# A Fourier mixing and maxout kernel on one core: one more split unit a batch, fewer and larger x fetches, evenly spaced scattered stores, and a re-cut first stage

## The chip, the cores and the metric

One NeuronCore of a Trainium2 chip runs the whole kernel. The metric is the device time of one execution in microseconds (us); lower is better. Five engines matter: TensorE (PE, matmuls into PSUM), VectorE (DVE), ScalarE (ACT), GpSimd (POOL), and SyncE (SP), which only issues DMAs here. POOL issues the loads of x and of the weights, which cast fp32 to bf16 on the way, and the scattered stores.

## The reference

x is 8 batches of 3072 rows of 256 numbers. The real part of a two-dimensional Fourier transform (over the 3072 rows and the 256 columns) is taken of each batch, and every resulting row of 256 goes through a maxout network with three input matrices and one output matrix.

```python
def _attn_ref(x):                      # x: (8, 3072, 256)
    X = np.fft.fft(x, axis=1)
    X = np.fft.fft(X, axis=2)
    return X.real.astype(np.float32)

def _moe_ref(x, w1, w2, w3, w_out):    # x: (24576, 256), w1..w3: (256, 768), w_out: (768, 256)
    h = np.maximum(np.maximum(x @ w1, x @ w2), x @ w3)
    return (h @ w_out).astype(np.float32)
```

Inputs and output are fp32; the kernel computes in bf16 with fp32 sums.

## The kernel before

**Algebra.** The transform over rows is done in two steps. Step s (`Mix.s`, lines 392 to 412) multiplies slices of x with a small table `tab`. The result goes through DRAM and back (`y`, `z`), or, for batch 0, through one DVE transpose (`t`, line 429). Step k (`Mix.k`, lines 456 to 466) multiplies with the tables `te_tab` and `to_tab` and gives `tE` and `tO`, the even and odd halves of the transform. Rows n and 3072 - n of the output share them, as a sum and a difference, so one unit of work makes both. The transform over the 256 columns is folded into the weights: `g_all` holds, for each of six chunks of 128 hidden columns, w2 - w1 and w3 - w1 in that form, even and odd part each, and `gd_all` holds multiples of the odd parts by a factor per partition (`dif`). Adding `gd_all` x `tO` to a plus sum turns it into the minus sum. `gw` and `g1t` carry the linear part (w1), which goes straight to the output.

**Units.** Each batch has 1536 row pairs in three blocks of 512 and six hidden chunks, so 18 units, numbered u = 0 to 17 inside a batch and g over all 144. The main loop (lines 880 to 917) takes one unit a turn. `begin` computes the plus side into `hp`, `finish` the minus side into `hm`, one unit later. There are two ways to do it:

- An unsplit unit has six matmuls of 512 columns: two each for two banks in `begin` (lines 485 and 486), and two in `finish` (line 492). ACT takes relu of one bank (`stmp`, line 498) and DVE the maximum with the other (line 499), once for each side.
- A split unit has five. `third`, called two units ahead, computes the even and the odd part of the w3 side into banks of their own (e and d, lines 841 and 843). ACT copies the odd part (line 845), DVE adds the correction `vb` x `wcol` to the even part (line 846), and POOL forms `plus` and `minus` in SBUF (line 850). `begin` then has two matmuls (lines 860 and 861) and `finish` one, and DVE takes both maxima (lines 862 and 874).

From g = 7 on, odd units are split. Even units are split where `EXTRA` says so, from batch 1 on: u = 0, 4, 8, and in the last batch also 14. The correction column `wcol` is made once, in unit 5 of batch 0 (`column`, lines 345 to 355), by 24 matmuls of one column.

**Second layer.** When a block's six chunks are done, `l2_block` is queued, and each unit runs ten steps of it, so a block's output appears during the next six units. DVE adds (line 577) into one of three output buffers (`obuf` and two halves of `kq`). Rows that lie regularly go out by SP (line 507). The mirrored rows go out as indirect stores issued by POOL (`scatter`, line 653), five per batch, which the main loop takes from the list `waiting`: one each at u = 8, 10 and 12 and two at u = 14. The last block of the last batch (`l2_last`, lines 584 to 617) is computed in flipped order instead, so that it needs no scatter; POOL makes the flipped tables (line 893) at unit 12.

**Plan.** Everything else is hung on units by `at(b, unit, fn)`: the k, s, y and z steps of the next batch, the loads of x three batches ahead, and the mirror copies of x (line 128, on ACT from batch 2 on, eight chunks at u = 5 to 12), which need both halves of the load (32 partitions each). The order of each engine's instructions is the order of this program; every queue is in order.

**First stage.** x of batch 0 comes in four chunks. DVE mirrors each (line 128); column 0 of the mirror is a copy of its own (line 132), by ACT for the first three chunks and by DVE for the last. s5 and s6 follow, DVE casts (line 403), DVE transposes, and then `m.k(0, 0, dve)` and `m.k(1, 0)` give the first 512 columns of `tE` (cast by DVE) and `tO` (cast by ACT), each in one PSUM bank of the pool `ps_f`. The pool `ps_s` of five banks serves this stage alone; the banks of the pools `ps_l1`, `ps_w3` and `ps_o`, which the units use, take its place afterwards.

**PSUM.** `ps_f` has three banks that e, d, the s and k steps and the linear part share in turn; `ps_l1` and `ps_o` have two each, `ps_w3` one. An even unit uses the `ps_w3` bank: as its second bank when it is unsplit, as its only one when it is split.

Of the kernel before, what the change touches and what calls it, by code (L numbers as in the profile page):

```python
# [9 lines left out]
FP32 = mybir.dt.float32  # L10
BF16 = mybir.dt.bfloat16
INT32 = mybir.dt.int32
UINT32 = mybir.dt.uint32
AX = mybir.ActivationFunctionType
# [13 lines left out]


FIRST_OF = (4, 8, 1)  # L30
EXTRA, EXTRA_LAST = (0, 4, 8), (0, 4, 8, 14)


def _parts(g):

    done = [(12 + i - 1, slice(128 * i + 96, 128 * i + 128)) for i in range(4)]
    for i in range(4 if g < 2 else 3):
        done.append((FIRST_OF[g] + i - 1, slice(128 * i, 128 * i + 96)))
    if g == 2:
        done += [(16, slice(384, 480, 2)), (15, slice(385, 480, 2))]  # L40
    return done
# [3 lines left out]
def kernel(  # L45
# [9 lines left out]
    nc = tc.nc  # L55

    B, S, D = x.shape
    assert (S, D) == (3072, 256)
    DFF = moe_w1.shape[1]
# [4 lines left out]
    NS = 49  # L64
# [6 lines left out]
    consts = ctx.enter_context(tc.tile_pool(name="consts", bufs=1))  # L71
# [20 lines left out]
    te_tab = consts.tile([128, NHALF + 1], BF16, tag="te_tab")  # L92
    to_tab = consts.tile([128, NHALF + 1], BF16, tag="to_tab")
    md_all = consts.tile([128, 512], BF16, tag="md_all")
    nmd_all = consts.tile([128, 512], BF16, tag="nmd_all")
    md = [md_all[:, fc * 256:(fc + 1) * 256] for fc in range(2)]
    nmd = [nmd_all[:, fc * 256:(fc + 1) * 256] for fc in range(2)]
    w1_bf = consts.tile([128, 2 * DFF], BF16, tag="w1_bf")
    w2_bf = consts.tile([128, 2 * DFF], BF16, tag="w2_bf")
    w3_bf = consts.tile([128, 2 * DFF], BF16, tag="w3_bf")  # L100
    wout_bf = consts.tile([128, NJC * 256], BF16, tag="wout_bf")
    g1t = consts.tile([128, NJC * 256], BF16, tag="g1t")
    g_all = consts.tile([128, 4 * DFF], BF16, tag="g_all")
    g_all = g_all.rearrange("p (c k j) -> p c k j", k=4, j=128)
# [11 lines left out]
    def load_x(b, s0, s1, h):  # L116

        rows = x[b].rearrange("(a s) d -> a s d", s=96)
        lo, hi = (s0, s1) if h == 0 else (max(s0, 1), min(s1, 48))
        src = rows[:, lo:hi, :] if h == 0 else rows[:, 97 - hi:97 - lo, :][:, ::-1, :]  # L120
        return nc.gpsimd.dma_start(out=xt[b % 2][32 * h:32 * h + 32, lo:hi, :], in_=src)  # L121

    def mirror(b, s0, s1):

        t = xt[b % 2]
        fn = (nc.vector.tensor_copy, (nc.gpsimd.tensor_copy, nc.vector.tensor_copy)[s0 >= 25],
              nc.scalar.copy)[min(b, 2)]
        fn(out=t[64:128, s0:s1, 1:128], in_=t[0:64, s0:s1, 255:128:-1])  # L128
        if b < 2:
            if b == 0 and s0 < 40:  # L130
                fn = nc.scalar.copy
            fn(out=t[64:128, s0:s1, 0], in_=t[0:64, s0:s1, 128])

    def mirror_first(b):

        t = xt[b % 2]
        nc.scalar.copy(out=t[64:128, :, 0], in_=t[0:64, :, 128])
# [3 lines left out]
    ps_s = ps_s_cm.__enter__()  # L141
# [52 lines left out]
    zero = gen.tile([128, 512], BF16, tag="zero")  # L194
    nc.vector.memset(zero, 0.0)
    nc.vector.memset(x0u, 0.0)
    half_pi = gen.tile([128, 1], FP32, tag="half_pi")
    nc.vector.memset(half_pi, 0.5 * math.pi)
    nc.scalar.activation(out=half_pi, in_=half_pi, func=AX.Sin)
# [4 lines left out]
    turn = gen.tile([128, 2], FP32, tag="turn")  # L204
# [10 lines left out]
    def scal(out, in0, s1, op0, s2=None, op1=None, eng=None):  # L215
        kw = {} if op1 is None else {"op1": op1}
        return (eng or nc.vector).tensor_scalar(out=out, in0=in0, scalar1=s1, scalar2=s2,
                                                op0=op0, **kw)
# [37 lines left out]
    dve = nc.vector.tensor_copy  # L256
    vm = gen.tile([128, 512], INT32, tag="vm")
# [16 lines left out]
    def wrap(c0, c1):  # L274
# [8 lines left out]
                          in_=par.unsqueeze(1).to_broadcast([128, 2, 2]))  # L283
# [42 lines left out]
    def differ(i0, i1, j0, j1):  # L326

        cs = slice(j0 // 128, j1 // 128)
        nc.vector.tensor_scalar(out=gd_all[:, cs, i0:i1, :], in0=g_all[:, cs, 2 * i0 + 1:2 * i1:2, :],
                                scalar1=dif, scalar2=None, op0=ALU.mult)  # L330
# [14 lines left out]
    def column():  # L345

        psc = ps_f.tile([128, 512], FP32, name="psc", tag="ps")
        for jc in range(NJC):
            for k, (table, wt) in enumerate(((md, w3_bf), (nmd, w1_bf))):
                for fc in range(2):  # L350
                    nc.tensor.matmul(psc[:, jc:jc + 1],
                                     wt[:, fc * DFF + jc * 128: fc * DFF + jc * 128 + 128],
                                     table[fc][:, 128:129],
                                     start=(k == 0 and fc == 0), stop=(k == 1 and fc == 1))
        nc.scalar.copy(out=wcol, in_=psc[:, 0:NJC])

    def prep_second():
# [143 lines left out]
    def stored(st, mine, others):  # L501
        for group in others:
            tc.declare_no_dep(st.ins, group=group, reason="each store has rows of its own")
        tc.add_to_no_dep_group(mine, st.ins)
# [144 lines left out]
    def scatter(n):  # L649

        for _ in range(min(n, len(waiting))):
            row, col, p0, p1, src = waiting.pop(0)
            stored(nc.gpsimd.indirect_dma_start(  # L653
                fours, bass.IndirectOffsetOnAxis(ap=rows_m[p0:p1, col:col + 1], axis=0),
                src, None, element_offset=256 * row), "scattered", ("scattered", "direct"))
            nc.gpsimd.memset(mark, 0.0)
# [11 lines left out]
    def warm_up(n):  # L668
        for _ in range(n):
            nc.tensor.matmul(warm, zero[:, 0:128], zero, start=True, stop=True)  # L670

    m = Mix(0)
# [11 lines left out]
    mirror(0, *FIRST[3])  # L684
    m.s(4, pool=ps_s)
    warm_up(2)
    scal(sgn, pidx, 0.0, ALU.is_equal)
    scal(sgn, sgn, 2.0, ALU.mult, -1.0, ALU.add)
    scal(dif, sgn, 1.0, ALU.subtract)
    m.s(5, pool=ps_s, evict=dve)  # L690
    nc.scalar.activation(out=md_all, in_=vm, func=AX.Sin, scale=float(2.0 * math.pi / 256.0),
                         bias=turn[:, 0:1])
    m.s(6, pool=ps_s)
    m.t()
    warm_up(2)
    nc.scalar.activation(out=nmd_all, in_=vm, func=AX.Sin, scale=float(-2.0 * math.pi / 256.0),
                         bias=turn[:, 1:2])
# [4 lines left out]
    for (s0, s1) in HALVES:  # L702
        for h in range(2):
            load_x(1, s0, s1, h)
        if s0 == 0:
            nc.gpsimd.dma_start(out=wout_bf.rearrange("p (jc c) -> p jc c", jc=NJC),
                                in_=moe_w_out.rearrange("(jc p) c -> p jc c", jc=NJC))
# [8 lines left out]
    table(1, 512, 1024)  # L716
    m.c(1, 16)
    warm_up(1)
    m.k(0, 0, dve)
    m.k(1, 0)  # L720
    differ(0, 2, 0, 128)
    keep(psg2, 1, 2, 128, 384, dve)
    differ(0, 2, 128, 384)
# [32 lines left out]
    def at(b, unit, fn):  # L756
        plan.setdefault((b + unit // UNITS, unit % UNITS), []).append(fn)
# [23 lines left out]
    def fetch(b, k):  # L781
        half, h = divmod(k, 2)
        load_x(b, *HALVES[half], h)

    def turn(b, ch):
        mirror(b, *EIGHTHS[ch])
# [14 lines left out]
        at(0, (3, 3, 4, 4)[ch], lambda ch=ch: mirror(1, *CHUNKS[ch]))  # L801
        at(0, 4, lambda ch=ch: fetch(2, ch))
    for b in range(2, B):
        for ch in range(4):
            if b > 2:
                at(b - 3, (9 + (b == 3), 11, 18, 19)[ch], lambda b=b, ch=ch: fetch(b, ch))
        for ch in range(8):
            at(b - 2, 5 + ch + 3 * (b == 2), lambda b=b, ch=ch: turn(b, ch))
        at(b - 2, 13 + 3 * (b == 2), lambda b=b: mirror_first(b))
# [70 lines left out]
    for g in range(B * UNITS):  # L880
        b, u = divmod(g, UNITS)
        blk, jc = divmod(u, NJC)
        mm = mixes[b]
        last = b == B - 1 and blk == 2
        if jc == 0:
            hp = h_pool.tile([128, NJC, TOKB], BF16, name="hp", tag="hp")
            hm = h_pool.tile([128, NJC, TOKB], BF16, name="hm", tag="hm")
            if last:
                flipped = []
                for t, name in ((mm.tE, "tEr"), (mm.tO, "tOr")):  # L890
                    fl = h_pool.tile([128, TOKB], BF16, name=name, tag=name)
                    flipped.append(fl)
                    nc.gpsimd.tensor_copy(fl, t[:, 3 * TOKB - 1: 2 * TOKB - 1: -1])
        if prev is not None and is_split(prev[0]) and not is_split(g):
            finish(*prev)
            prev = None
        pses = begin(g, hp[:, jc, :])
        if prev is not None:
            finish(*prev)
        prev = (g, pses, hm[:, jc, ::-1] if last else hm[:, jc, :])  # L900
        for lead in (1, 2):
            if is_split(g + lead) and (lead == 1) == (g + lead == 7):
                third(g + lead)
        scatter({8: 1, 10: 1, 12: 1, 14: 2}.get(u, 0))
        l2_some(10)
        if b == B - 1 and u in (1, 3):
            if u == 1:
                middle = l2_mid()
            next(middle, None)
        for fn in plan.get((b, u), ()):  # L910
            fn()
        if jc == NJC - 1:
            l2_some(1000)
            if g == B * UNITS - 1:
                finish(*prev)
            l2_queue.append(l2_last(hp, hm, mm.tE, mm.tO, flipped) if last else
                            l2_block(b, blk, hp, hm, mm.tE, mm.tO))
# [32 lines left out]
```

## Time and profile before

| what | value |
|---|---|
| median of 3 runs | 392.28 us (392.26 to 392.38) |
| the profiled execution | 391.42 us, its span 389.3 us |
| mean granted TensorE clock | 0.998 |
| PE busy | 376.2 us (97% of the span) |
| DVE, POOL, ACT busy | 327.7, 314.3, 248.4 us |
| one batch in the middle | 44.28 us |
| POOL plus and minus, each | 1.27 us, 91 of each |
| scattered stores on POOL | 37, 1.0 us each |

The span runs from the first to the last instruction; the execution's time has 2.1 us around it. A matmul's row shows its whole passage through the array (380 ns for 512 columns), and consecutive ones overlap, so what a matmul costs is read from start to start. A row of the timeline gives start, duration, engine, line, operation, output and inputs; the bracket at its end is the idle time of that engine before it and what ended it.

### The profile page before, as it was taken

Reading aid. Unit: us, or ns where it says so; the run is one execution under the profiler, and the core shown is the slowest. Engines: PE = TensorE matmul, PEld = TensorE weight load, DVE = VectorE, ACT = ScalarE, POOL = GpSimd, SP = SyncE. Lnnn points to the kernel's source line nnn. Section 1 sums busy time; section 2 is a strip of 40 time slices with the busy share of each in tenths; the row PEclk is TensorE's granted clock in tenths of the full one; section 3 lists DMA queues with packets and bytes.
Section 4 is the critical chain, followed back from the end, with each engine's and each line's share of the span. In section 5 each row is a group of like instructions: output and inputs, shape, how many; then the busy total and the mean of one; then the engine's idle time right before and its main releaser. Section 6 shows DMA issues by size and latency. Waiting matters only on the chain.

```text
span 389.3 us, 8092 instructions
## 1 busy us (share of the span) xinstructions
PE 376.2 (97%) x2817; PEld 236.2 (61%) x2817; DVE 327.7 (84%) x552; ACT 248.4 (64%) x453; POOL 314.3 (81%) x363
## 2 busy tenths in 40 slices
PE   6699999999999999999999999999999999999985
PEld 2355566566665666566665666656665666666654
DVE  7788797799797988899797988989887997999972
ACT  6877789567856696567856687567866346434420
POOL 9983576879898898879898898879787887769881
PEclk9999999999999999999999999999999999999999
DMA  7999764585747666475938657575423544212226
GB/s 113 184 183 160 163 145 118 112 168 161 178 141 130 172 176 154 111 128 186 189 120 149 169 151 176 125 128 185 113 94 93 149 138 139 70 31 80 85 89 206
DMA packets 52263, 54.13 MB, mean 139 GB/s; under 512 B 26547, under 2 KB 45009, under 8 KB 51367
## 3 DMA queue, kind: packets, MB, share of 16 engines
q0 software_dynamic: 20272, 26.45, 34.4%
q1 hardware_dynamic: 31418, 26.58, 25.0%
q10 hardware_dynamic: 532, 0.59, 0.5%
q8 instruction: 22, 0.36, 0.3%
q14 instruction: 19, 0.16, 0.1%
HBM read 36.95 MB, written 30.81 MB: 174 GB/s over the span
## 4 chain that ended last, share of the span: by engine, by line
PE 87%; POOL 4%; DVE 4%; DMA 2%; ACT 1%; issue 1%; DVEq 0%; POOLq 0%
PE po L549 30%; PE pse L492 10%; PE pse L860 5%; PE pse L485 5%; PE pse L486 5%; PE d L843 5%; PE e L841 5%; PE pse L861 5%; PE po L572 5%; PE ps L461 3%; PE ps L396 3%; PE pl L565 2%; DMA xt<-in_x_dram 2%; POOL xt L121 1%; POOL plus L850 1%
## 5 line engine op out<-in xcount | busy, mean ns | idle before, releaser
L850 POOL TENSOR_TENSOR plus<-even,odd 128x512 bf16<-128x512 f32 x91 | 115.7, 1271 | 55.4 <-DVE even L846 44.1
L850 POOL TENSOR_TENSOR minus<-even,odd 128x512 bf16<-128x512 f32 x91 | 115.5, 1269 | 0.0
L845 ACT ACTIVATE odd<-d 128x512 f32<-128x512 f32 x91 | 54.4, 598 | 55.8 <-PE d L843 41.9
L862 DVE SCALAR_TENSOR_TENSOR hp<-pse,plus 128x512 bf16<-128x512 f32 x91 | 62.6, 688 | 32.2 <-PE pse L861 27.9
L549 PE MATMUL po<-wout_bf,hp 128*128 128x256 bf16 x576 | 86.1, 273 | 0.0
L498 ACT ACTIVATE stmp<-pse 128x512 bf16<-128x512 f32 x106 | 63.2, 600 | 24.2 <-PE pse L486 11.2
L549 PE MATMUL po<-wout_bf,hm 128*128 128x256 bf16 x576 | 78.6, 273 | 0.0
L549 PEld LDWEIGHTS <-hp 128*128 128x128 bf16 x576 | 56.3, 98 | 26.2
L492 PE MATMUL pse<-tO,gd_all 128*128 128x512 bf16 x197 | 66.1, 380 | 1.3 <-DVE hp L862 1.3
L846 DVE SCALAR_TENSOR_TENSOR even<-vb,wcol,e 128x512 f32<-128x512 bf16 x91 | 67.1, 737 | 0.0
L549 PEld LDWEIGHTS <-hm 128*128 128x128 bf16 x576 | 56.3, 98 | 16.4
L874 DVE SCALAR_TENSOR_TENSOR hm<-pse,minus 128x512 bf16<-128x512 f32 x91 | 61.9, 680 | 0.4
L499 DVE TENSOR_TENSOR hp<-pse,stmp 128x512 bf16<-128x512 f32 x53 | 36.4, 686 | 8.8 <-ACT stmp L498 4.2
L499 DVE TENSOR_TENSOR hm<-pse,stmp 128x512 bf16<-128x512 f32 x53 | 36.5, 689 | 6.7 <-ACT stmp L498 4.3
L485 PE MATMUL pse<-tE,g_all 128*128 128x512 bf16 x106 | 40.2, 379 | 0.8 <-DVE tE L463 0.4
L577 DVE TENSOR_TENSOR kq<-po,even 128x512 f32<-128x512 f32 x60 | 40.9, 682 | 0.0
L128 ACT COPY xt<-xt 64x762 bf16<-64x762 bf16 (+1 forms) x48 | 39.8, 838 | 1.0
L486 PE MATMUL pse<-tO,g_all 128*128 128x512 bf16 x106 | 40.2, 379 | 0.0
L572 PE MATMUL po<-gw,tO 128*128 128x512 bf16 x92 | 34.9, 379 | 0.0
L860 PE MATMUL pse<-tE,g_all 128*128 128x512 bf16 x91 | 34.6, 380 | 0.1
L653 POOL DMA_INDIRECT out_dram<-kq,rows_m x29 | 29.0, 1000 | 6.8 <-issue 5.7
L841 PE MATMUL e<-tE,g_all 128*128 128x512 bf16 x91 | 34.5, 379 | 0.0
(173 smaller groups left out, 511.7 us busy)
## 6 DMA issues: line engine op xcount, KB each, us to landing
xt<-in_x_dram POOLq DMA_DIRECT2D x14, 384.0 KB
db<-tb SPq DMA_DIRECT2D x21, 192.0 KB
out_dram<-obuf SPq DMA_DIRECT2D x8, 384.0 KB
out_dram<-kq SPq DMA_DIRECT2D x8, 384.0 KB
vb<-vd SPq DMA_DIRECT2D x23, 128.0 KB
xt<-in_x_dram POOLq DMA_DIRECT2D x7, 400.0 KB
xt<-in_x_dram POOLq DMA_DIRECT2D x7, 368.0 KB
out_dram<-kq SPq DMA_DIRECT2D x7, 288.0 KB
```

What stands on the lines that cost most here:

```text
L485: nc.tensor.matmul(pse[:, 0:n], g_all[:, jc, 2 * i, :], te, start=True, stop=False)
L486: nc.tensor.matmul(pse[:, 0:n], g_all[:, jc, 2 * i + 1, :], to, start=False, stop=True)
L492: nc.tensor.matmul(pse, gd_all[:, jc, i, :], to, start=False, stop=True, skip_group_check=True)
L498: nc.scalar.activation(out=stmp[:, 0:n], in_=pses[0][:, 0:n], func=AX.Relu)
L499: nc.vector.tensor_tensor(out=dst, in0=src3, in1=stmp[:, 0:n], op=ALU.max)
L549: nc.tensor.matmul(po, hcols(jc), wout_bf[:, jc * 256:(jc + 1) * 256], start=False, stop=(jc == NJC - 1), skip_group_check=True)
L572: nc.tensor.matmul(po, to[:, cp], gw[:, 256:768], start=True, stop=True)
L845: nc.scalar.activation(out=odd3, in_=d3, func=AX.Copy, scale=-0.5)
L846: nc.vector.scalar_tensor_tensor(out=even3, in0=vb, scalar=wcol[:, jc:jc + 1], in1=e3, op0=ALU.mult, op1=ALU.add)
L850: nc.gpsimd.tensor_tensor(out=dst, in0=even3, in1=odd3, op=op)
L862: nc.vector.scalar_tensor_tensor(out=dst, in0=pse2, scalar=0.0, in1=sums[g][0], op0=ALU.max, op1=ALU.max)
L874: nc.vector.scalar_tensor_tensor(out=dst, in0=pses[0], scalar=0.0, in1=sums.pop(g)[1], op0=ALU.max, op1=ALU.max)
```

## The change

- `EXTRA` and `EXTRA_LAST` are both (0, 4, 8, 12): unit 12 is split too in batches 1 to 7, and in the last batch unit 14 is not split any more. There are 97 split units instead of 91.
- The scattered stores go one at a time, at u = 0, 4, 8, 12 and 14 (`PACE`), and in the last batch also at u = 16.
- From batch 3 on, x is fetched in two pieces instead of four: all 49 rows of the first 32 partitions at unit 13 of the batch three before, and the 47 rows of the next 32 partitions at unit 18, which is unit 0 of the batch after.
- In the first stage, column 0 of the last mirror chunk is copied by POOL instead of DVE; the three small operations that make `sgn` and `dif` come after the transpose on DVE instead of before the s5 cast; and the first 512 columns of `tE` and `tO` are computed by `k_first`: two banks of 256 columns for each table, taken from `ps_s`, the first cast by DVE, the second by ACT.
- `column` reads row 0 of `g_all[:, jc, 3, :]` with a one-by-one tile `one`: six matmuls of one column instead of 24.

```diff
+PACE = (0, 4, 8, 12, 14)
-EXTRA, EXTRA_LAST = (0, 4, 8), (0, 4, 8, 14)
+EXTRA, EXTRA_LAST = (0, 4, 8, 12), (0, 4, 8, 12)
...
         if b < 2:
-            if b == 0 and s0 < 40:
-                fn = nc.scalar.copy
+            if b == 0:
+                fn = nc.scalar.copy if s0 < 40 else nc.gpsimd.tensor_copy
             fn(out=t[64:128, s0:s1, 0], in_=t[0:64, s0:s1, 128])
...
+    one = consts.tile([1, 1], BF16, tag="one")
+    nc.vector.memset(one, 1.0)
...
         for jc in range(NJC):
-            for k, (table, wt) in enumerate(((md, w3_bf), (nmd, w1_bf))):
-                for fc in range(2):
-                    nc.tensor.matmul(psc[:, jc:jc + 1],
-                                     wt[:, fc * DFF + jc * 128: fc * DFF + jc * 128 + 128],
-                                     table[fc][:, 128:129],
-                                     start=(k == 0 and fc == 0), stop=(k == 1 and fc == 1))
+            nc.tensor.matmul(psc[:, jc:jc + 1], g_all[0:1, jc, 3, :], one, start=True, stop=True)
...
     warm_up(2)
+    m.s(5, pool=ps_s, evict=dve)
+    nc.scalar.activation(out=md_all, in_=vm, func=AX.Sin, scale=float(2.0 * math.pi / 256.0),
+                         bias=turn[:, 0:1])
+
+    def k_first(which):
+
+        for h in range(2):
+            ps2 = ps_s.tile([128, 512], FP32, name="ps2", tag="ps")
+            for (i, cols) in _parts(0):
+                at = cols.start - 256 * h
+                if 0 <= at < 256:
+                    nc.tensor.matmul(ps2[:, at:at + cols.stop - cols.start], m.col(i, which),
+                                     (te_tab, to_tab)[which][:, cols], start=True, stop=True)
+            (dve, nc.scalar.copy)[h](out=(m.tE, m.tO)[which][:, 256 * h:256 * h + 256],
+                                     in_=ps2[:, 0:256])
+
+    m.s(6, pool=ps_s)
+    m.t()
     scal(sgn, pidx, 0.0, ALU.is_equal)
     scal(sgn, sgn, 2.0, ALU.mult, -1.0, ALU.add)
     scal(dif, sgn, 1.0, ALU.subtract)
-    m.s(5, pool=ps_s, evict=dve)
-    nc.scalar.activation(out=md_all, in_=vm, func=AX.Sin, scale=float(2.0 * math.pi / 256.0),
-                         bias=turn[:, 0:1])
-    m.s(6, pool=ps_s)
-    m.t()
...
-    m.k(0, 0, dve)
-    m.k(1, 0)
+    k_first(0)
+    k_first(1)
...
-        for ch in range(4):
+        for h in range(2):
             if b > 2:
-                at(b - 3, (9 + (b == 3), 11, 18, 19)[ch], lambda b=b, ch=ch: fetch(b, ch))
+                at(b - 3, (13, 18)[h], lambda b=b, h=h: load_x(b, 0, NS, h))
...
-        scatter({8: 1, 10: 1, 12: 1, 14: 2}.get(u, 0))
+        if u in PACE or (b == B - 1 and u == 16):
+            scatter(1)
```

## The prediction

> **What bounds the kernel now.** I read the page first, then the busy time by stretches, the timeline of each engine around every place that the diff touches, and last the end of the chain of waits.
>
> ```profile
> span 389.3 us, 8092 instructions
> PE 376.2 (97%) x2817; PEld 236.2 (61%) x2817; DVE 327.7 (84%) x552; ACT 248.4 (64%) x453; POOL 314.3 (81%) x363
> ```
>
> ```profile
> core 0: us, PE busy (x) PEld busy (x) DVE busy (x) ACT busy (x) POOL busy (x), PEclk, DMA share, GB/s
> 20.00:43.50 23.50, 22.44 (x179) 12.61 (x179) 18.35 (x35) 18.04 (x38) 13.52 (x27) 1.00 1.08 173
> ...
> 205.72:250.00 44.28, 44.28 (x334) 28.01 (x335) 38.24 (x61) 30.91 (x55) 38.16 (x40) 1.00 0.65 153
> ...
> 366.00:378.00 12.00, 10.66 (x72) 6.82 (x71) 9.26 (x16) 3.23 (x6) 11.15 (x13) 1.00 0.20 67
> ```
>
> In a middle batch PE is busy for all of its 44.28 us at full clock: a matmul taken away there is time taken away, as long as DVE (38.24) and POOL (38.16) keep up. Near the end PE has holes while POOL is full, and the chain of waits says who makes them:
>
> ```profile
> 368.27 0.69 DVE hp L862
> 368.96 0.18 issue
> 369.13 0.89 POOL out_dram L653
> ...
> 370.11 1.25 POOL plus L850
> 371.36 1.21 POOL minus L850
> 372.57 0.20 issue
> 372.77 1.12 POOL out_dram L653
> ...
> 374.19 0.98 POOL out_dram L653
> ...
> 375.26 1.25 POOL plus L850
> 376.52 0.02 issue
> 376.54 0.70 DVE hp L862
> ```
>
> Here three scattered stores and the sums of units 14, 15 and 17 stand in one POOL queue, and DVE's hp of 15 and 17 starts 0.03 us after its plus. And at the start:
>
> ```profile
> 13.37 0.55 DVE L128 COPY xt<-xt 64x1143 bf16<-64x1143 bf16 x1 [0.97 <-DMA xt<-in_x_dram]
> ...
> 13.84 0.16 DVE L132 COPY xt<-xt 64x9 bf16<-64x9 bf16 x1
> ...
> 14.06 0.41 PE L396 MATMUL ps<-xt,tab 128*64 128x512 bf16 x2 [0.62 <-DVE xt L132]
> ```
>
> **Split of unit 12.** An unsplit unit has six 512-column matmuls, a split one five (e and d in `third`, two in `begin`, one in `finish`). They start 0.216 us apart (341.51, 341.73, 341.95). Batches 1 to 6 gain one split unit each: 6 x 0.216 = 1.30 us off PE. Batch 7 trades 14 for 12: nothing.
> The cover: each new split adds on POOL plus and minus, 1.27 + 1.27 less 0.04 of overlap = 2.5 us, on DVE one even (0.66 from start to start), on ACT 0.60 less 2 x 0.60. POOL around units 10 to 13 (rows from 226 us): the sums of 11 end at 228.60; today a fetch (0.56) and a scattered store (0.96, with mark and gaps 1.5) follow. Both leave that place, so the sums of 12 end near 231.5 and those of 13 near 234.0, 0.7 later than today's 233.3; hp of 13 keeps 0.5 of its 1.15 to 1.34 us of slack. From unit 15 POOL is where it was. DVE, in the batch from 161 us: hp of 10 at 182.94, the new even at 183.55, then 0.6 more for each that follows, hm of 10 at 185.40 instead of 184.84, done 186.09. Unit 12 now opens on the bank that this hm frees; PE wants it at 186.23 (185.80 plus two matmuls of the new third). Cover of 0.1 us: it holds, or costs up to 0.2 a batch, as unit 8 pays already (221.58 after hm's end at 221.52, 0.11 lost). I take 0.03 a batch: **-1.1** (from -1.3 to 0).
>
> **Weight column.** The 24 one-column matmuls start 0.025 apart (two per 0.05: 35.06, 35.11); 18 fewer are 0.45 us. Behind them psw feeds DVE's gw copy (37.17, idle 0.28 before it), then ACT, hp, even and the first plus; DVE can move up by 0.35 only (it is held by hm at 36.21), and PE waits for that chain at 43.28 and 45.56 (0.12 and 0.28). **-0.37** (-0.45 to -0.2).
>
> **First stage.** The column-0 copy of the last chunk goes from DVE (0.16) to POOL, behind four iotas, the last of which ends at 13.89. POOL's copies of 12 and 13 columns took 0.23, so it ends near 14.07 to 14.12 and PE's s5 starts at 14.12 to 14.18 rather than 14.06; were POOL free it could start 0.09 earlier. Queued behind the copy on POOL are the last weight loads, 0.25 later; their matmuls come at 21.68, and the copy of the next x at 25.81 has 0.7 us before PE's 29.82. sgn and dif (14.03 to 14.56) lay beside PE's s5 and now lie between the transpose's end (19.08) and the first cast (19.61): free in both places.
> Halved casts: 256 columns take 0.42 on DVE (row L606), on ACT about 0.37 (587 for 512 columns, 478 for 384). By transpose-end times of today tO would be whole at about 20.33 instead of 20.54. But the four half banks are the ones that the first units' pse inherit, and in the built order the first pse matmul now waits for DVE and ACT and the second for nobody: it waits for all four casts. So it starts at 20.39 instead of 20.36, and the second at 20.61 instead of 20.59. The early first half buys nothing. Together **+0.08** (-0.15 to +0.3).
> A row that bears on the moved copy: the 128x1 iota at 13.49 beside DVE's copy took 401 ns, the other 128x1 iotas 121. The Trainium skill, "SBUF — State Buffer", section "SBUF: two separate sides", has GpSimd blocked while a DVE copy holds the port pair they share, until about 0.115 us after its end. By that page the copy would end near 14.25, the step would cost 0.25 and the sum would come out 0.2 higher; the row fits it, but the iota ended with DVE's copy and the POOL copy stands behind it anyway.
>
> **Two fetches for four, paced stores.** POOL saves two issues a batch (0.56 + 0.78), off the path. The fetch of the first 32 partitions, at unit 13, starts near 238.3 and is not needed before 260. The other, 47 rows, moves from units 11 and 19 to unit 18: it goes behind a store that is new there (249.2 to 250.2), is issued near 250.5, and pushes the sums of unit 3 back 0.8 us, which have 2.78. Its 1504 packets: 736 took 3.25 us after a lead of 1.5 (issue 252.92, last 257.68), so it lands near 258.5. ACT reads it first at 260.56 (216.27 plus a batch). Cover 2 us, price under the rivals. Behind it on the DMA engines wait the y writes, read at unit 12. Stores at units 0, 4, 8 and 12 fall into POOL idle times (the store at 4 into 1.7 us before the sums of 7), and their buffers are rewritten five or more units later. Taken at 0.
>
> **The end.** Batch 7 has POOL work of 14 moved to unit 10, and the double store of unit 14 becomes one there and one at 16. Redone with the rows: sums of 13 end 365.9, flips 367.1, store 368.3, plus of 15 ends 369.6 (now 371.35) and is wanted at 369.45; store to 372.2, plus of 17 ends 373.6 and is wanted at 374.0. PE's matmuls start late there by 0.92 (371.11 to 372.14 is 1.03, a 256-column one takes 0.11), 0.13, 0.15 and 0.75: 1.95 us. I take **-1.8** (-0.9 to -1.95). What is late next is PE itself, then DVE's hm of 17, 0.4 us ahead of its reader. What follows the last matmul (384.7 to 389.3) stays.
>
> **Sum:** -1.1 - 0.37 + 0.08 - 1.8 = -3.2 us. The profiled execution took 391.42 (span 389.3 and 2.1 around it), 0.86 under the median of the runs, 392.28. I take the same step from the median: 389.1.
>
> **Rivals.**
> 1. The cover is used up. Speaking for it: 0.1 us for unit 12's bank, and a plus wanted 0.15 before it is there at unit 15. Against: PE has no other hole in the middle batches. Splits give 0, one of the two end stalls (0.75) stays: -0.37 + 0.08 - 1.05 = -1.3, or 391.0. Chance 0.19.
> 2. Slower: the large fetch lands late. The slowest row is 768 packets in 4.9 us after 1.65 (issue 233.26, last 239.81, beside other loads); 1504 at that pace behind the store's data land near 262.1, 1.5 late. ACT is in order, so stmp of unit 6 waits behind the mirror copy; 0.4 us of idle absorbs some, 1.1 us reach PE, five times: +5.5 - 3.2, or 394.6. It decides once the fetch needs over 10 us from issue. Against: at this point of the batch the rows are the fast ones. Chance 0.08.
> 3. The first stage does not do what it says: all four casts are waited for. That is in the sum already, inside the forecast's chance; were it wrong, the second pse matmul could start at 20.39, -0.2 more: 388.9.
>
> **Chances.** Forecast 0.68 (its own range 388.2 to 390.0), rival 1 0.19, rival 2 0.08, the rest between them 0.05. Range 388.2 to 391.2. Over 0.2% (0.8 us, about what a measurement of this kernel can tell from none) faster 0.86, within 0.05, slower 0.09.
>
> **What would show it.** Right: middle batches of 44.07 us with PE full; hp of 12 behind PE and not POOL; no PE hole over 0.3 us between 360 and the last matmul; psc of six; the first pse matmul within 0.1 of 20.4. Wrong: ACT's mirror copy waiting for the x DMA, a hole before unit 12's first matmul, or plus still releasing hp of 15 and 17.

## The result, and the profile after

After takes 388.17 us (median of five, 387.95 to 388.44) against 392.28 us before: a ratio of 0.9893, interval 0.9879 to 0.9908, or 4.1 us less. The forecast was 389.1 with a low end of 388.2, so the direction and most of the size were right and the time came out 0.03 us below the range. The two profiled executions differ by less than the medians: 391.42 to 388.44, 2.98 us. Most of the experiments are about that difference.

The page of after, its span and its busy times:

```profile
span 386.5 us, 8006 instructions
...
PE 371.5 (96%) x2744; PEld 235.6 (61%) x2793; DVE 331.9 (86%) x559; ACT 246.0 (64%) x448; POOL 324.2 (84%) x366
```

PE has less to do and DVE and POOL have more, as intended. (A few matmul records are missing from each trace, so the counts are not exact.) A middle batch, in the busy times by stretches of after (the stretch, its length, then the busy time of each engine):

```profile
core 0: us, PE busy (x) PEld busy (x) DVE busy (x) ACT busy (x) POOL busy (x), PEclk, DMA share, GB/s
...
205.50:249.57 44.07, 43.64 (x328) 27.91 (x330) 38.87 (x63) 30.51 (x54) 39.49 (x42) 1.00 0.66 154
```

The stretch from one batch's s step to the next is 44.07 us instead of 44.28. The 0.4 us that PE's busy time lacks here is where matmuls have no record: 328 rows are counted where 333, one fewer than before's 334, are due. The same step of the next batch starts at 117.31, 161.38, 205.44, 249.51 and 293.57: every batch gains the full 0.216 us.

At the end of batch 7 the chain of waits no longer has POOL or DVE in it. After's chain:

```profile
369.62 0.66 PE po L547 x6
...
371.35 0.66 PE po L547 x6
...
372.71 0.59 PE pse L490 x2
373.30 1.09 PE po L547 x10
...
374.83 0.66 PE po L547 x6
```

POOL's own timeline of after for the same time shows why: one store, sums, one store, sums, and only then the third store.

```profile
366.00 0.87 POOL L651 DMA_INDIRECT out_dram<-kq,rows_m  x1 [0.17 <-issue]
...
366.92 1.27 POOL L861 TENSOR_TENSOR plus<-even,odd 128x512 bf16<-128x512 f32 x1
...
369.60 1.13 POOL L651 DMA_INDIRECT out_dram<-kq,rows_m  x1 [0.20 <-issue]
...
370.79 1.27 POOL L861 TENSOR_TENSOR plus<-even,odd 128x512 bf16<-128x512 f32 x1
...
373.45 0.98 POOL L651 DMA_INDIRECT out_dram<-obuf,rows_m  x1 [0.17 <-issue]
```

The plus of 17 ends at 372.06, in before at 376.51: 4.45 us earlier, while the matmul for which PE waited there in before starts 3.05 us earlier (374.23 instead of 377.28). So the plus ends 1.4 us further ahead of that matmul than in before, and PE has no hole there.

The first stage came out later than forecast in this profile. Its timeline:

```profile
13.51 0.60 DVE L129 COPY xt<-xt 64x1143 bf16<-64x1143 bf16 x1 [0.99 <-DMA xt<-in_x_dram]
14.14 0.22 POOL L133 COPY xt<-xt 64x9 bf16<-64x9 bf16 x1
14.41 0.41 PE L394 MATMUL ps<-xt,tab 128*64 128x512 bf16 x2 [0.85 <-POOL xt L133]
```

PE's s5 starts at 14.41 against 14.06 before. 0.14 of this is x landing later, and 0.21 is the longer way from DVE's copy to s5 (0.90 instead of 0.69). And the large fetches, in after's list of DMA issues (KB each, then median us from issue to landing):

```profile
xt<-in_x_dram POOLq DMA_DIRECT2D x5, 784.0 KB, 8.3
xt<-in_x_dram POOLq DMA_DIRECT2D x5, 752.0 KB, 7.9
```

7.9 us is within the 10 us that ACT's mirror copies allow (the slowest of these five took 8.9); in this trace they never waited for it.

### The profile page after: what moved, and what is told of

The parts are those of the page before. It is cut to its first block, busy times and chain, and to the rows that moved or that the text cites. A ratio compares the mean times of both kernels' runs of the same rounds, so it can differ in the third digit from the quotient of the medians.

```text
span 386.5 us, 8006 instructions
## 1 busy us (share of the span) xinstructions
PE 371.5 (96%) x2744; PEld 235.6 (61%) x2793; DVE 331.9 (86%) x559; ACT 246.0 (64%) x448; POOL 324.2 (84%) x366
## 4 chain that ended last, share of the span: by engine, by line
PE 88%; POOL 4%; DVE 3%; issue 2%; ACT 1%; DVEq 0%; POOLq 0%
PE po L547 32%; PE pse L490 11%; PE e L852 6%; PE d L854 5%; PE pse L871 5%; PE po L570 5%; PE pse L872 5%; PE pse L484 5%; PE pse L483 4%; PE ps L459 3%; PE ps L394 3%; PE pl L563 3%; POOL xt L122 1%; POOL w_bf L184 1%; DVE yb L427 1%
## 5 line engine op out<-in xcount | busy, mean ns | idle before, releaser
L861 POOL TENSOR_TENSOR plus<-even,odd 128x512 bf16<-128x512 f32 x97 | 123.1, 1269 | 43.9 <-DVE even L857 36.8
L861 POOL TENSOR_TENSOR minus<-even,odd 128x512 bf16<-128x512 f32 x97 | 123.0, 1268 | 0.0
L857 DVE SCALAR_TENSOR_TENSOR even<-vb,wcol,e 128x512 f32<-128x512 bf16 x97 | 71.5, 737 | 0.0
L496 ACT ACTIVATE stmp<-pse 128x512 bf16<-128x512 f32 x94 | 56.0, 600 | 21.9 <-PE pse L490 10.3
L885 DVE SCALAR_TENSOR_TENSOR hm<-pse,minus 128x512 bf16<-128x512 f32 x97 | 66.0, 681 | 0.8 <-PE pse L484 0.4
L497 DVE TENSOR_TENSOR hp<-pse,stmp 128x512 bf16<-128x512 f32 x47 | 32.3, 687 | 8.0 <-ACT stmp L496 4.6
L854 PE MATMUL d<-tO,gd_all 128*128 128x512 bf16 x97 | 36.8, 379 | 0.0
L497 DVE TENSOR_TENSOR hm<-pse,stmp 128x512 bf16<-128x512 f32 x47 | 32.3, 688 | 4.7 <-ACT stmp L496 2.9
L567 ACT COPY even<-pl 128x512 f32<-128x512 f32 x46 | 26.8, 583 | 11.4 <-DVE kq L575 7.8
L484 PE MATMUL pse<-tO,g_all 128*128 128x512 bf16 x86 | 32.6, 379 | 0.6 <-issue 0.2
```

Source lines behind the costliest of these rows:

```text
L496: nc.scalar.activation(out=stmp[:, 0:n], in_=pses[0][:, 0:n], func=AX.Relu)
L497: nc.vector.tensor_tensor(out=dst, in0=src3, in1=stmp[:, 0:n], op=ALU.max)
L854: nc.tensor.matmul(d3, gd_all[:, jc, 1, :], to, start=True, stop=True)
L857: nc.vector.scalar_tensor_tensor(out=even3, in0=vb, scalar=wcol[:, jc:jc + 1], in1=e3, op0=ALU.mult, op1=ALU.add)
L861: nc.gpsimd.tensor_tensor(out=dst, in0=even3, in1=odd3, op=op)
L885: nc.vector.scalar_tensor_tensor(out=dst, in0=pses[0], scalar=0.0, in1=sums.pop(g)[1], op0=ALU.max, op1=ALU.max)
```

## The experiments

Two names are used below. "The middle" is the stretch from PE's s5, its first matmul on the last x chunk, to the start of its last matmul; "the tail" is from there to the end of the span. Both come from PE's rows in the trace of each run. Runs of before that stood beside these kernels had medians of 392.29, 392.17, 392.47 and 392.19 us in four groups of 17.

### Where before's own times differ

The kernel before, unchanged, with more times and more profiles.

> The kernel before, once more, with five times and a second profile. What is to be told apart is why the medians moved by 4.1 us (392.28 to 388.17) while the two profiled executions moved by 2.98 (391.42 to 388.44). Theory 1 (a lucky start): the profiled execution of before had its first x chunks early; here times of 391.4 to 392.6, and a profile near 392.3 would carry the extra 0.9 us ahead of PE's first unit, at 45.95 us. Theory 2 (the end varies): the POOL-bound end of batch 7 is longer in most executions; a profile near 392.3 would read 45.95 as before and the extra 0.9 behind 360 us. Theory 3 (something outside the span): the span stays at 389.3 and the time around it is 3 us instead of 2.1.

> The kernel before, a third profile. The first two have PE's last matmul at 384.44 and 384.42 and spans of 389.3 and 389.9; the runs of before have spans of 389.7 to 391.1, median 390.2. Theory 1 (only the last stores vary): the last matmul again at 384.4, and a span from 389.3 to 391 that differs only behind it. Theory 2 (PE loses time now and then in the middle, by transfers that land late): the last matmul later than 384.6 where the span is 390.3 or more.

> The kernel before, a fourth profile; the theories and their numbers are those of the third.

> The kernel before, a fifth profile, to see inside an execution with a span of 390.5 or more. Theory 1 (start and last stores only): the stretch from PE's matmul on the last x chunk to its last matmul is 370.4 as in the four others, and the rest is ahead of it (up to 0.8) or behind it (5.5 to 6.5). Theory 2 (PE loses time in between now and then): that stretch is 370.7 or more.

> The kernel before, a sixth profile; theories and numbers are those of the fifth.

> The kernel before, a seventh profile; theories and numbers are those of the fifth.

> The kernel before, an eighth profile; theories and numbers are those of the fifth.

Measured: 392.26 us (12 runs, 391.80 to 393.63), ratio 1.0003 [0.9993, 1.0013]. The eight profiles of before, in us:

| profile | s5 starts | middle | tail | span | time |
|---|---|---|---|---|---|
| the one shown before | 14.06 | 370.38 | 4.9 | 389.3 | 391.42 |
| before_again | 14.06 | 370.36 | 5.5 | 389.9 | 392.02 |
| look 2 | 13.72 | 370.36 | 6.0 | 390.1 | 392.21 |
| look 3 | 13.89 | 370.47 | 5.5 | 389.9 | 391.95 |
| look 4 | 14.37 | 370.41 | 5.4 | 390.1 | 392.25 |
| look 5 | 14.07 | 370.37 | 5.4 | 389.8 | 391.89 |
| look 6 | 14.42 | 370.38 | 6.2 | 391.0 | 393.07 |
| look 7 | 14.46 | 370.37 | 5.2 | 390.0 | 392.15 |

The middle is 370.4 in all eight (median 370.37), whatever the span, so theory 1 of looks 4 to 7 holds. The time around the span is 2.1 us in each, so theory 3 of before_again falls. What varies is the landing of the first x (s5 from 13.72 to 14.46, with the loads issued at the same times to 0.02 us) and the tail (4.9 to 6.2, mean 5.5). The profile that the forecast was made from has the shortest tail of the eight.

The busy times by stretches show where the tail is made. These are the two microseconds from 4 to 2 us ahead of the last matmul's start (the last two columns are the DMA share and GB/s). First the profile shown before:

```profile
380.40:381.40 1.00, 1.00 (x11) 0.90 (x10) 0.21 (x1) 0.00 (x0) 0.00 (x0) 1.00 0.91 348
381.40:382.40 1.00, 1.00 (x11) 0.90 (x10) 0.48 (x1) 0.00 (x0) 0.22 (x1) 1.00 0.90 369
```

Then look 6, the longest of the eight:

```profile
380.80:381.80 1.00, 1.00 (x12) 0.90 (x10) 0.25 (x1) 0.00 (x0) 0.00 (x0) 1.00 0.88 266
381.80:382.80 1.00, 1.00 (x12) 0.90 (x10) 0.44 (x1) 0.00 (x0) 0.27 (x1) 1.00 0.92 307
```

And after:

```profile
377.40:378.40 1.00, 1.00 (x12) 0.90 (x10) 0.26 (x1) 0.00 (x0) 0.00 (x0) 1.00 0.86 320
378.40:379.40 1.00, 1.00 (x12) 0.90 (x10) 0.43 (x1) 0.00 (x0) 0.27 (x1) 1.00 0.93 373
```

The stores are issued at the same times ahead of the last matmul in all profiles of before, and the DMA engines are equally busy, but look 6 moves 0.14 MB less in these two microseconds. It has that left when the very last stores arrive. The last packet of POOL's own DMA queue (queue 0) ends 3.4 us after the last matmul's start in look 6, instead of 2.1, and in each of the eight profiles the span ends 2.7 to 2.9 us after that packet.

The other traces bear this out. The six other profiles of before move 0.57 to 0.60 MB in the same two microseconds, as look 6 does; the one shown before is the exception with 0.7. Over all 18 profiles on record that issue every store, those that move 0.69 MB or more there have tails of 4.65 to 5.18 us, and those that move 0.60 or less have 5.22 to 6.17.

### after_again

> After, once more. Four profiles of before have from the start of PE's last matmul to the end 4.9, 5.5, 6.0 and 5.5 us; the one the forecast was made from has the least. Theory 1 (that stretch is shorter in after): 4.6 to 5.2 us here, spans of 386.1 to 386.6, a spread under 0.7 us. Theory 2 (chance: after varies as before does): a stretch up to 6 us, spans up to 387.5, and a median over more runs nearer to 388.6.

Measured: 388.09 us (387.89 to 388.36), ratio 0.9889 [0.9874, 0.9905], spans 386.1 to 386.6. s5 at 14.36, middle 367.00, tail 4.8. Theory 1 holds: the tail is 5.15 and 4.84 in after's two profiles, 4.65 to 5.18 in four kernels below with the same end, and the spread is half a microsecond (5 runs) where before_again had 1.8 (12 runs). The spread says less than the tail: one_more_split and copy_back_whole_casts, with the same end, have 2.1 and 1.8.

### before_fewer_stores and after_fewer_stores

```diff
-    scatter(len(waiting))
+    waiting.clear()
     l2_some(1000)
```

The rows of the last scattered store stay unwritten in both kernels. The store holds 128 rows of 1024 fp32 numbers, 512 KB and not the 192 KB of the expectations; queue 0 moves 0.52 MB less without it.

> Before, with the last scattered store left out (192 KB, issued 5.7 us before the last matmul starts; those rows of the output stay unwritten), and nothing else. PE's part is the same. Theory 1 (the stretch behind the last matmul is as long as what the DMA engines still hold when the last stores are issued): 4.0 to 4.9 us instead of 5.5 to 6.0, 391.2 to 391.6 beside 392.2, with less spread. Rival (its length is that of the very last stores alone): 392.1 to 392.3, the spread as before.

> After, with its last scattered store left out (192 KB, issued 6.0 us before the last matmul starts; those rows of the output stay unwritten). Theory 1 (in after the DMA engines have caught up before the very last stores, so that the stretch behind the last matmul is at its floor): 4.7 to 5.1 us, the time of after to 0.15, 387.95 to 388.1. Rival (this store lengthens the stretch in after as it does in before): -0.4 to -0.6, 387.5 to 387.7.

Measured in before: 391.86 us (391.18 to 392.40), ratio 0.9986 [0.9976, 0.9996], middle 370.37, tail 4.98. The same two microseconds in its trace:

```profile
380.80:381.80 1.00, 1.00 (x11) 0.89 (x10) 0.23 (x1) 0.00 (x0) 0.00 (x0) 1.00 0.55 205
381.80:382.80 1.00, 1.00 (x12) 0.89 (x10) 0.46 (x1) 0.00 (x0) 0.25 (x1) 1.00 0.00 0
```

The DMA engines run empty (share 0.00) and the tail is still 5.0: that is about the floor, set by the last stores themselves. Theory 1 is right in kind and too hopeful in size (a tail of 4.98 against 4.0 to 4.9, 391.86 against 391.2 to 391.6). The spread is a little less, 1.2 us (12 runs) instead of about 1.5 (17). Measured in after: 388.09 us, ratio 0.9894 [0.9876, 0.9913], tail 5.17. Nothing gained: after is at this floor already.

### end_alone and end_split_only

```diff
-EXTRA, EXTRA_LAST = (0, 4, 8), (0, 4, 8, 14)
+EXTRA, EXTRA_LAST = (0, 4, 8), (0, 4, 8, 12)
...
-        scatter({8: 1, 10: 1, 12: 1, 14: 2}.get(u, 0))
+        if b == B - 1:
+            scatter(u in (0, 4, 8, 12, 14, 16))
+        else:
+            scatter({8: 1, 10: 1, 12: 1, 14: 2}.get(u, 0))
```

end_split_only has the first of the two edits alone.

> Before, with the change of batch 7 alone: unit 12 split there in place of 14, and stores at units 0, 4, 8, 12, 14 and 16 of that batch. Theory 1 (sum of the steps): -1.9 us beside before (the trace of after shows -1.94), so a ratio near 0.9951. Theory 2 (before's end varies and is longer in most executions than in the profiled one): -2.6 to -2.9, ratio 0.9927 to 0.9934, and a narrower spread of the five times than before has.

> Before, with unit 12 of batch 7 split in place of 14, and the stores of that batch where they were, two of them behind unit 14. By the rows of before the sums of 14 (2.5 us) leave the queue ahead of those of 15 and 17, so plus of 15 ends 0.6 ahead of its reader and plus of 17 at 374.0, when it is wanted. Theory 1 (the moved split does it, the spread stores only keep it): the stretch up to the last matmul 368.4 to 368.6, and a ratio of 0.9940 to 0.9955. Rival (the double store is as much to blame): 369.2 to 369.6, ratio 0.9965 to 0.9980. The stretch behind the last matmul: 5.0 if it hangs on PE's holes at the end, 5.5 if on where the stores are.

end_alone: 389.97 us (389.46 to 391.17), ratio 0.9943 [0.9929, 0.9957]. The middle is 368.43, 1.94 less than before; the tail is 4.95. The median lies between the two theories: the middle gives what theory 1 says and the tail adds to it.

end_split_only: 391.52 us (390.87 to 393.92), ratio 0.9987 [0.9972, 1.0001], middle 369.74, only 0.63 less. Theory 1 falls, and the rival was too hopeful too. POOL's timeline of this kernel:

```profile
358.75 1.27 POOL L850 TENSOR_TENSOR plus<-even,odd 128x512 bf16<-128x512 f32 x1 [0.20 <-issue]
...
364.13 0.91 POOL L653 DMA_INDIRECT out_dram<-kq,rows_m  x1
...
368.86 0.88 POOL L653 DMA_INDIRECT out_dram<-kq,rows_m  x1 [0.17 <-issue]
...
371.01 1.27 POOL L850 TENSOR_TENSOR minus<-even,odd 128x512 bf16<-128x512 f32 x1
372.47 1.13 POOL L653 DMA_INDIRECT out_dram<-kq,rows_m  x1 [0.19 <-issue]
...
373.90 0.98 POOL L653 DMA_INDIRECT out_dram<-obuf,rows_m  x1 [0.21 <-DVE kq L577]
...
374.94 1.28 POOL L850 TENSOR_TENSOR plus<-even,odd 128x512 bf16<-128x512 f32 x1
```

The sums of 14 are gone, yet the plus of 17 starts at 374.94 instead of 375.23. The sums of 12 have come in ahead of it, so between the plus of 11 (the first row) and that of 17 stand the sums of four units and four stores, as many as in before. PE's hole of 0.75 us before 17 stays. In end_alone only two stores stand there:

```profile
358.58 1.27 POOL L850 TENSOR_TENSOR plus<-even,odd 128x512 bf16<-128x512 f32 x1 [0.57 <-DVE even L846]
...
367.25 0.88 POOL L653 DMA_INDIRECT out_dram<-kq,rows_m  x1 [0.15 <-DVE even L846]
...
370.87 1.13 POOL L653 DMA_INDIRECT out_dram<-kq,rows_m  x1 [0.19 <-issue]
...
372.05 1.28 POOL L850 TENSOR_TENSOR plus<-even,odd 128x512 bf16<-128x512 f32 x1
```

From plus to plus it is 13.47 us there and 16.19 here: two stores fewer are worth 2.7 us of POOL's queue. The bracket of the fourth store names DVE, but that wait cost next to nothing: 0.21 us of idle time, where stores that wait for nothing have 0.15 to 0.20. On top of the moved split the stores bring 1.3 of the 1.94 us gained at the end, and the moved split by itself 0.63; the stores by themselves were not run.

### splits_alone

```diff
-EXTRA, EXTRA_LAST = (0, 4, 8), (0, 4, 8, 14)
+EXTRA, EXTRA_LAST = (0, 4, 8, 12), (0, 4, 8, 14)
```

> Before, with unit 12 split in batches 1 to 6 and nothing else: four fetches a batch as they were, stores at units 8, 10, 12 and 14, batch 7 untouched. Theory 1 (the freed POOL time at units 10 and 11 is not what the split needs): -1.3 us, ratio 0.9967, middle batches of 44.07. Rival (the cover hangs on the fetch and the store that left units 10 and 11): the sums of 12 come 2.1 us later, at about 233.6 on the clock of before's profile, hp of 12 and what follows wait for them, PE loses 0.2 or more a batch, and the time is that of before or more (ratio 1.000 or above).

Measured: 391.06 us (390.24 to 391.57), ratio 0.9964 [0.9949, 0.9978], middle 369.25, 1.12 less. PE loses 0.2 us once, before unit 12's first matmul at 230.17, in one batch of six. The cover holds even with the old fetches and stores in the way, and the rival's price is 0.2 us a run, not 0.2 a batch.

### one_more_split

```diff
-EXTRA, EXTRA_LAST = (0, 4, 8, 12), (0, 4, 8, 12)
+EXTRA, EXTRA_LAST = (0, 4, 8, 12, 16), (0, 4, 8, 12)
```

> After, with unit 16 of batches 1 to 6 split too (batch 7 as it is). It takes 0.216 us a batch off PE and adds 2.5 us of sums to POOL, which has about 40.5 of the 44.07 us of a batch. Theory 1 (POOL's total is what counts): POOL 43.0 of 43.85, it holds, -1.3 us, 386.9. Theory 2 (the order on POOL counts, and units 14 to 17 with a store and the flips ask for 2.5 us a unit of 2.44): PE waits 0.3 or more a batch for hp of 16 and 17, and the time is 388.5 to 391.

Measured: 388.33 us (387.53 to 389.64), ratio 0.9894 [0.9874, 0.9915]: the time of after, within what is measured. Middle 367.07 against 367.00, tail 5.2. Its busy times by stretches, and what PE waited for:

```profile
205.50:249.57 44.07, 43.53 (x327) 27.67 (x329) 38.80 (x63) 29.63 (x53) 41.46 (x42) 1.00 0.67 154
```

```profile
PE pse L871 <- DVE hm L497: 0.5, 1, 0.5
```

Neither theory's price is right. In this profile the split takes its 1.3 us off PE and PE loses as much again. The largest single loss is 0.70 us at 220.62, before an even unit's first matmul, which waits for the hm that frees its bank. What made that hm late stands on ACT:

```profile
216.77 0.82 ACT L129 COPY xt<-xt 64x762 bf16<-64x762 bf16 x1 [1.30 <-DMA xt<-in_x_dram]
...
220.06 0.60 ACT L496 ACTIVATE stmp<-pse 128x512 bf16<-128x512 f32 x1
```

ACT waited 1.30 us for x: the fetch issued at 206.07 landed 10.7 us later, and the chain of waits goes from ACT's copies and stmp to that hm and to PE. This is rival 2 of the forecast, once, and just past the 10 us that it names. This is the only trace on record in which one of ACT's mirror copies for the later batches waits for x. The other losses are 0.14 us in each of four batches and 0.23 once, at 333; no wait is named for them, and they are what a cover nearly used up would look like. The profiled run, 388.96, belongs to the longer half of the six: three took 387.5 to 387.8 and three 388.9 to 389.6. So the median does not show that the split gives nothing. Where the fetch lands in time it may gain some 0.4 us (an estimate, from the three shorter runs against after's 388.1 to 388.2); there is no profile of such a run.

### column_alone

```diff
-            for k, (table, wt) in enumerate(((md, w3_bf), (nmd, w1_bf))):
-                for fc in range(2):
-                    nc.tensor.matmul(psc[:, jc:jc + 1], ...
+            nc.tensor.matmul(psc[:, jc:jc + 1], g_all[0:1, jc, 3, :], one, start=True, stop=True)
```

> Before, with the weight column by six matmuls out of the table that is there already, and nothing else. Theory 1 (18 matmuls fewer, most of it reaches the end): -0.27 us (after's trace) to -0.37 (the forecast), a ratio of 0.9991 to 0.9993. Rival (PE waits at 43 and 46 us for a chain that does not move): 0 (ratio 1.0000).

Measured: 391.43 us (12 runs, 391.02 to 392.21), ratio 0.9984 [0.9976, 0.9993], which takes in theory 1 at its edge. The middle is 370.06, 0.31 less than before, and the profile has the start of look 2 to 0.01 us, so that the two can be compared row by row: the last matmul starts at 383.78 and 384.08.

### four_fetches

```diff
-        for h in range(2):
-            if b > 2:
-                at(b - 3, (13, 18)[h], lambda b=b, h=h: load_x(b, 0, NS, h))
+        for ch in range(4):
+            if b > 2:
+                at(b - 3, (9 + (b == 3), 11, 18, 19)[ch], lambda b=b, ch=ch: fetch(b, ch))
```

> After, with x of each later batch in four fetches at the units of before (9 or 10, 11, 18 and 19), and the rest as in after. Theory 1 (the fetches are worth nothing, as the sum had them): the time of after, 388.2, middle batches of 44.07. Theory 2 (two fetches for four are where the rest of the 4.1 us comes from): 388.6 to 389.0. Rival (the fetch of unit 11 stands ahead of the sums of 12 and 13): 0.1 to 0.5 a batch on PE, 388.8 to 391.

Measured: 388.51 us (388.06 to 388.85), ratio 0.9903 [0.9888, 0.9917], which overlaps that of after. The middle is 366.85, 0.14 less than after: the two fetches cost PE one loss of 0.14 us at 69.30, in batch 1, which this kernel does not have. But what lies around the span is 2.15 us here and 1.86 in after (medians of the runs), so that the time is no better. By the median alone, theory 1 and the low end of theory 2 cannot be told apart; PE's part speaks for theory 1.

### copy_back and copy_back_whole_casts

```diff
-                fn = nc.scalar.copy if s0 < 40 else nc.gpsimd.tensor_copy
+                fn = nc.scalar.copy if s0 < 40 else nc.vector.tensor_copy
```

and for the second kernel also

```diff
-    k_first(0)
-    k_first(1)
+    m.k(0, 0, dve)
+    m.k(1, 0)
```

> After, with the column-0 copy of the last x chunk back on DVE and the rest as it is. Theory 1 (the copy on POOL starts only when DVE's copy has ended, and runs longer there): -0.15 to -0.2 us beside after, 387.95 to 388.05, and PE's s5 0.69 after the start of DVE's copy instead of 0.90. Rival (the start has slack that takes it up): the time of after, 388.2, with the first pse matmul no earlier.

> After, with the column-0 copy back on DVE and the first tables in whole casts (DVE 512 columns, ACT 512 columns) as in before. Theory 1 (halves bought nothing, since the first two pse matmuls wait for all four of them): the first pse matmul 1.28 us after the transpose's end as in before, and the time of copy_back, 388.2. Rival (the early halves did help): the first pse matmul 1.5 or more behind the transpose, and 388.4 or more.

Measured: 388.21 us (387.99 to 388.59), ratio 0.9896 [0.9881, 0.9910], and 388.29 us (387.60 to 389.38), 0.9897 [0.9879, 0.9914]. Both are the time of after. Halves or whole, s5 is followed by the first pse matmul 6.29 to 6.33 us later, as in before (6.28 to 6.32). The copy did not come out shorter on DVE. The first stage in copy_back:

```profile
13.23 0.76 DVE L129 COPY xt<-xt 64x1143 bf16<-64x1143 bf16 x1 [0.79 <-DMA xt<-in_x_dram]
13.92 0.47 DVE L133 COPY xt<-xt 64x9 bf16<-64x9 bf16 x1
14.44 0.41 PE L394 MATMUL ps<-xt,tab 128*64 128x512 bf16 x2 [0.95 <-DVE xt L133]
```

The nine columns take 0.47 us here, against 0.16 to 0.20 in seven profiles of before and 0.41 in look 4, and s5 starts 1.21 us after DVE's copy begins. The second kernel shows the same (0.47 and 1.28). Theory 1 of copy_back falls. None of the kernels beats after beyond what is measured.

## Why the prediction was right in kind and 0.03 us outside its range

**The sum was right.** From s5 to the last matmul the forecast had -1.1 - 0.37 - 1.8 = -3.27 us. Eight profiles of before and two of after give 370.4 and 367.0: -3.39. Part by part:

| part | forecast | measured on PE | from |
|---|---|---|---|
| six splits | -1.1 | -1.3 | batch of 44.07; -1.12 alone, with the old fetches |
| column | -0.37 | -0.31 | column_alone |
| end of batch 7 | -1.8 | -1.94 | end_alone |
| fetches, stores | 0 | +0.14 | four_fetches |

The four measured parts add up to -3.4. The first and the last are read in after itself, beside four_fetches; with the -1.12 of splits_alone in the first place it is -3.2, so up to 0.2 us of the splits' gain hangs on the old fetches and stores having left. The 0.03 us a batch that was put aside for unit 12's bank was not needed.

**The step that failed** is the last: "What follows the last matmul (384.7 to 389.3) stays", and with it taking the step from the profiled execution over to the median. Those 4.9 us were read in one execution, and it was the luckiest of eight. In a usual execution of before the tail is 5.5 us, because the DMA engines still hold earlier stores when the last ones come: without one of these stores the tail was 4.98 and the median of the runs lower by 0.2 to 0.9 us (the interval of before_fewer_stores). After's tail is 5.0, about the floor that both kernels have without the store in question (4.98 and 5.17). So the change shortens the tail by 0.5 us in a usual execution, and not at all beside the profile that was shown (4.9 to 5.15).

That after no longer carries this remainder is shown. Why is only argued: the three stores before the last ones are issued 0.25 us earlier ahead of the last matmul (POOL's 6.0 instead of 5.7 us ahead). All seven profiles with the earlier issue moved 0.69 to 0.72 MB in the two microseconds looked at above; of the eleven with the old issue times three did (the one shown before, column_alone and end_split_only). end_split_only has a tail of 5.0 in its one profile, but its median moved no more than its middle did. No run moved the issue times alone.

**A second constant** that was none: the time around the span. The forecast carried 2.1 us over. It is 2.1 in before and 1.8 to 1.9 in after, copy_back and their like, 2.15 with four fetches and 2.3 with one more split, and 1.8 to 2.1 within the five runs of splits_alone. No run shows what sets it. Together, with the means of the profiles: middle -3.39, tail -0.5, around the span -0.25, s5 later by 0.22 (14.13 in eight profiles of before, 14.35 in the five with POOL's copy, of which 0.20 is x landing later), which makes -3.9 of the 4.1 us. The last 0.2 is within what so few profiles can tell. Of the 0.9 us by which the forecast's -3.2 fell short, 0.5 is the tail, 0.25 the time around the span and 0.1 the middle; s5, 0.14 later than forecast, works against it, and 0.2 stays open.

**First stage**, +0.08. In the first profile the way from DVE's copy to s5 grew by 0.21. Over all profiles it is 0.90, 0.78, 0.87, 0.59 and 0.58 with POOL's copy and 0.67 to 0.88 in the eight of before: +0.02 on the mean (0.74 and 0.73), so a cost of this step is not shown. The rule that was weighed there, the Trainium skill, "SBUF — State Buffer", section "SBUF: two separate sides", agrees in kind: POOL's copy never ends before DVE's copy does. But three of the five profiles have it start 0.03 to 0.04 us after the end of DVE's copy instead of 0.115, and in the other two its row runs beside DVE's copy and ends 0.02 us after it (in four_fetches from 13.88 to 14.28, where DVE's copy ends at 14.27). The halved casts bought nothing, as forecast. The mark "first pse matmul within 0.1 of 20.4" was missed (20.70), because x landed late there; before itself has 20.00 to 20.74.

**Weight column.** PE's rows of after have the six:

```profile
35.48 0.30 PE L352 MATMUL psc<-one,g_all 1*128 1x1 bf16 x6
35.71 1.05 PE L372 MATMUL psw<-wout_bf,g1t 128*128 128x256 bf16 x8
```

The stall behind it at 45.6 us stayed (0.28), as forecast, and so the full 0.45 was not to be had.

**Rivals.** The slower one, the fetch that lands late, had 7.9 us in after against the 10 from which it would decide (8.9 at most). It did come in one_more_split: one fetch landed after 10.7 us and cost PE 0.70. Rival 1, the cover used up, did not come with unit 12: every batch gained its 0.216. With the next split PE loses 0.14 us in four of the six batches. The other marks of the forecast came as written: batches of 44.07, no PE hole over 0.3 us between 360 and the last matmul, plus no longer releasing hp of 15 and 17.

## What to carry to other kernels

One profile is one draw: compare its own time with the times of the other runs before anything in it is taken for constant, above all the first loads and the last stores, which vary while the middle repeats to 0.1 us. A store in an in-order queue costs those behind it its own time in the queue (two were worth 2.7 us here), so moving stores may be worth more than moving the arithmetic beside them (1.3 us on PE against 0.63 here). Arithmetic that is moved within the queue, from one place ahead of the work that is waited for to another, takes nothing out of its way. When a median lies between two groups of runs, as in one_more_split, ask of the profile which group it belongs to before it is taken for the cause.

## What was not expected of the hardware

- The middle, some 370 us, repeats to 0.1 us over eight executions, while the first 14 us vary by 0.7 and what follows the last matmul (4.9 to 6.2) by 1.3.
- At the same DMA share (0.9) the same kernel moved 348 and 369 GB/s in one execution and 266 and 307 in another, at the same place.
- DVE's copy of nine columns took 0.16 to 0.20 us in ten of the 15 profiles that have it, and 0.35 to 0.47 in five (look 4, before_fewer_stores, end_split_only and the two copy_back kernels). In these five POOL had begun to issue a weight load 0.31 to 0.38 us before the copy, and the copy ended with that issue, to 0.01 us. In four of the ten such an issue had begun 0.27 us before the copy, and the copy took 0.16 to 0.17. Why the few hundredths decide is open.
- The time around the span differs by up to 0.5 us between kernels that differ in a fetch or a split (1.8 to 2.3).
